# A masked-attention and rational-FFN kernel: a gate on weight loads, GpSimd planned as one queue, earlier norms, and a new table of order numbers

## The chip, the cores and the metric

The kernel runs on one core of a Trainium2 chip. Its time is the device time of one execution in microseconds, and the time of a version is the median of its runs. The core's engines run at the same time, each in the order of its own instruction list: TensorE (PE, with its weight loads PEld), VectorE (DVE), ScalarE (ACT), GpSimd (POOL), and SyncE (SP), which here only issues transfers. An instruction that must wait holds back all that stands behind it on its engine. Transfers are issued from the lists of SP, ACT and GpSimd, and the 16 DMA engines carry them out.

## The reference: what is computed

Eight batches with eight heads each, 576 positions and a head width of 64. In every row of scores only those within `tau` of the row's maximum take part in the softmax. The attention output, 4608 tokens by 512, goes through a two-layer network (512 to 2048 and back) whose nonlinearity is a rational function:

```python
scores = scale * np.matmul(q, k.transpose(0, 1, 3, 2))
thresh = np.max(scores, axis=-1, keepdims=True) - tau
scores = np.where(scores >= thresh, scores, -1000000000.0)
attn = np.exp(scores - np.max(scores, axis=-1, keepdims=True))
attn = attn / (np.sum(attn, axis=-1, keepdims=True) + 1e-09)
x = np.matmul(attn, v)          # then heads side by side: (4608, 512)
h = x @ w_in
P = a[0] + a[1] * h + a[2] * h * h + a[3] * h * h * h
Q = 1.0 + np.abs(b[0]) * np.abs(h) + np.abs(b[1]) * h * h
out = (P / (Q + 1e-06)) @ w_out
```

## The kernel before, in words

**The attention half.** Work goes in units: one pair of heads (32 pairs, four to a batch) and one tile of 128 query rows, or the last 64 rows of both heads. For each unit PE multiplies Q by K (L874 to L885), DVE takes the row maxima from PSUM (L891, L893), a small step on DVE or ACT makes the threshold (L900 or L898), ACT masks (L906) and exponentiates with a row sum (L910), DVE and ACT make the reciprocal (L915 or L917, then L921). Each probability row is then split into a high float16 half (`hi`, through the helper `times`, L341 on ACT or L343 on DVE) and a low one (L932, DVE). Both are transposed by DMA from SP (L942), and PE multiplies them with V (L1003). The first pairs go another way, with a float32 transpose on PE (L955, L960) and a copy out of PSUM (L333 or L335). The result, split into `x` high and `x` low (L1013 or L1015, L1019), is the input of the network.

**The network half.** It works on chunks of 256 tokens: two chunks to a batch, and one for the remainder rows of four batches. A chunk is done in steps of eight feature tiles (`moe_ops`). A step's first layer is L1248 on PE; ACT evacuates it (L1258); DVE and ACT evaluate the rational function (L1265 or L1267, L1273 to L1299); its value is scaled and split into a high half (L341 on ACT or L343 on DVE, with the scale `gsc`) and a low half (L1313, DVE); the second layer is L1322 on PE. The matmuls use float16 halves, three products for one.

**The norm chain.** Before the high and low halves of a chunk's first step can be made, the scale `gsc` of the chunk must be known, and it comes from a bound on the values. This is a chain over four engines, `norm_ops`, `bound`, `floor_ops`, `gain`: squares of `x` (L1107 on ACT or L1109 on DVE), a sum over them on PE (L1114), a maximum and a root on DVE (L1117, L452, L453), seven tiny instructions in a row on GpSimd (L1130 to L1136), two tiny ones on DVE (L1141, L1142), and two more on GpSimd (L1176 writes `gsc`, L1177; L1155 and L1156 for the first batch). Each has one value per partition. There are 18 such chunks, and 20 passes through the GpSimd part, since the chunks of the first batch are done for each half of the weights.

**GpSimd's list.** GpSimd does these tiny steps, clears some corners of the V tiles (L787), and issues the weight loads (L584, L634, 16 of them with 1 MB each) and, for the pairs from the ninth on, the loads of Q, K and V (L714 to L725, L758, L762), and most stores of the output (L1345, L1349). Its program order is one list.

**Who sets the order.** Nothing is ordered by hand. Every step is an `Op` with the engines that may do it, a cost on each, a key, and what it waits for; `Plan.order` lays all of them out on a model of the engines and so fixes, before anything runs, each engine's list and which engine does the flexible steps (`FLEX`, weighed by `START`, `EARLY` and `PRICE`). A key is the place of the unit or step plus a number from the table `K`. In the model before, GpSimd's arithmetic (`POOL`) and the transfers that it issues (`GD`) are two engines, though on the chip both stand in one list, and the two GpSimd parts of the norm chain cost 1.6 and 0.4. The norm chain of a chunk has the key of its first step less 0.1 (`norm_ops(ck, p - 0.1)`); a unit of the key is about one attention unit.

**The gate.** `decode_ops` holds back a weight load by an extra GpSimd instruction that reads the load `AHEAD` places earlier, if that one was issued less than `RECENT` before in the model; the condition is on L522. With `AHEAD = 3` and `RECENT = 9.0` it never applies, and no such instruction is in the program.

Of the kernel before, what the change touches and what calls it, by code (L numbers as in the profile page):

```python
# [30 lines left out]

LEAD, SPACE0, SPACING = 4.291, 6.563, 3.948
ENDK, ENDS = 2.754, 33.74

WHEN = [(-0.303, 2.09), (4.753, 1.193), (9.83, -0.311), (12.579, -0.299)]

V0, V1 = 2.109, -9.048

SINGLE = 18

# [3 lines left out]
LAST = (2, 0, 1)  # L44
SOON = 1

NB = 8
# [25 lines left out]

AHEAD_RANK = 3.973

AHEAD = 3

RECENT = 9.0

# [7 lines left out]

K = {"f1": 1.261, "f2": -0.32, "f4": -0.218, "f6": 0.826, "load": -1.146, "junk": 1.219, "sq": 0.474, "cn": -0.3, "cs": 0.443,
     "s1": 1.268, "s2": 0.713, "wh": 0.93, "wl": 0.588, "wc": -0.225, "vl": 0.197, "vc": 0.201, "vh": 0.137, "qk": 0.035,
     "max": -0.025, "thr": -0.477, "pre": -0.921, "sum": 1.315, "rec": -0.226, "rec2": 0.027, "diag": -1.496, "tr": 0.586,  # L90
# [4 lines left out]

SHIFT_STEPS, SHIFT_UNITS = {}, {}

START = {"ACT": 3.357, "DVE": 3.139}
START_END = 100.161
EARLY = {"ACT": 2.148, "DVE": 3.18}  # L100
EARLY_END = 1301.58
PRICE = {"ACT": 2.362, "DVE": 1.311}

TOL = {"PE": 0.11, "ACT": 0.025, "DVE": 0.0, "POOL": 0.1, "DMA": 0, "GD": 0}
WARM, WARM_END = 0.6, 400.0
# [29 lines left out]
class Plan:  # L135
# [21 lines left out]
    def op(self, eng, dur, key, fn, after=(), take=(), drop=()):  # L157
        engs = {eng: dur} if isinstance(eng, str) else eng
        o = Op(engs, key + self.shift, fn, [x for x in after if x is not None], list(take), list(drop))
        o.rank, o.tiling = self.rank, "ff"  # L160
        self.ops.append(o)
        return o
# [20 lines left out]
    def order(self):  # L183
# [21 lines left out]
        while left:  # L205
# [29 lines left out]
            t, o, e = best  # L235
# [13 lines left out]
            free[e] = end = t + o.dur  # L249
            busy[e] += o.dur  # L250
            if e == "PE":
                tiling = o.tiling[1]
# [39 lines left out]
def masked_attention_rational_ffn(  # L292
# [852 lines left out]
    def first_gain(ck, i, key):  # L1145
        j = index(ck)
        w = gt[:, j, :] if i == 0 else gt[:, NK + ck[2], :]

        def f():
            if i:  # L1150
                nc.gpsimd.tensor_scalar(w[:, 1:2], gt[:, j, 1:2], 1.0, 1.0, ALU.mult, ALU.mult)
            bound(w, isx[:, 0:1], sg[:, i:i + 1])

        def f_out():
            nc.gpsimd.tensor_scalar(gsc[:, j, i:i + 1], w[:, 5:6], 2.0 ** UPG, 1.0, ALU.mult, ALU.mult)  # L1155
            nc.gpsimd.tensor_scalar(osc_[:, j, i:i + 1], w[:, 4:5], su[:, 2 * NH + i:2 * NH + i + 1], 1.0, ALU.mult, ALU.mult)  # L1156
        plan.rank = key
        o = op("POOL", 1.6, key, f, [norm_done[ck], half_done[i]])
        return op("POOL", 0.4, key, f_out, [floor_ops(w, key, o)])

    def gain(ck, key):
# [16 lines left out]
        plan.rank = key  # L1178
        o = op("POOL", 1.6, key, f, [norm_done[ck], ready_all])
        return op("POOL", 0.4, key, f_out, [floor_ops(w, key, o)])  # L1180

# [24 lines left out]
    def moe_ops(ck, f0, nb, p, begins, ends, soon):  # L1206
# [11 lines left out]
        if ck not in norm_done:  # L1218
            norm_ops(ck, p - 0.1)
        if (ck, fh if first else 0) not in gsc_done:  # L1220
# [308 lines left out]
```

## Time and profile before

| | |
|---|---|
| median of 3 runs | 1341.53 us (1337.87 to 1342.36) |
| profiled execution | 1342.67 us |
| its span, first to last instruction | 1340.9 us |
| mean granted TensorE clock | 0.968 |
| HBM traffic | 63.25 MB read, 9.44 MB written |

The profiled execution lies 0.09% above the median, so sums made against it hold for the median as well; 1.8 us lie around its span. In the rows of the profile "busy" is time in which the engine works, and the waits are idle time put down to what ended it: "DVE gt L1141 <- POOL gt L1136: 35.0, 18, 3.7" says that DVE stood idle ahead of its instruction of line 1141 until the GpSimd instruction of line 1136 was done, 35.0 us in all, 18 times, at most 3.7 us. A timeline row gives start, duration, engine, line, and in brackets the idle time before it.

### The profile page before, as it was taken

The page shows a single profiled execution, that of the slowest core. Times are in us where ns is not written, and L with a number is a line of the kernel's source. Part 1 is how long each engine was busy: PE and PEld are TensorE (multiplying, and loading weights), DVE is VectorE, ACT ScalarE, POOL GpSimd, SP SyncE. Part 2 cuts the span into 40 slices and gives each one's busy share as a digit, 9 for nine tenths or more (in the row PEclk, how much of TensorE's full clock was granted, in tenths as well). Part 3 has the DMA queues.
Part 4 walks back from the last instruction along what each step waited for, and adds up shares of the span by engine and source line. Part 5 has one row for each costly group of instructions (what it writes and reads, how often), then busy time and mean ns, then how long its engine had stood idle before and what let it go on. Part 6 is the DMA issues. An engine that isn't in the chain of part 4 may idle for free.

```text
span 1340.9 us, 25552 instructions
## 1 busy us (share of the span) xinstructions
PE 1236.1 (92%) x9540; PEld 802.3 (60%) x9540; DVE 1220.4 (91%) x1789; ACT 1112.9 (83%) x2111; POOL 336.6 (25%) x663
## 2 busy tenths in 40 slices
PE   6689899999899989999999999989899999899996
PEld 5556656666566655565656565646565656566752
DVE  4699879999899899999999999989999999999875
ACT  3799778999899889888989798979889889896442
POOL 2010202013322331333224142142413441420110
PEclk8898989999999989999999999989899999999998
DMA  8253125568557865475545575566656875652000
GB/s 297 57 207 123 28 55 111 91 130 160 108 119 133 141 109 121 86 150 117 124 89 105 85 151 108 116 118 125 143 90 116 159 147 117 125 98 52 17 17 16
DMA packets 338987, 149.61 MB, mean 112 GB/s; under 512 B 314560, under 2 KB 320944, under 8 KB 338864
## 3 DMA queue, kind: packets, MB, share of 16 engines
q1 hardware_dynamic: 316240, 87.14, 37.1%
q0 software_dynamic: 22304, 60.25, 16.2%
q8 instruction: 75, 1.23, 0.4%
q10 hardware_dynamic: 320, 0.59, 0.2%
q14 instruction: 48, 0.39, 0.1%
HBM read 63.25 MB, written 9.44 MB: 54 GB/s over the span
## 4 chain that ended last, share of the span: by engine, by line
DVE 27%; PE 18%; ACT 7%; issue 6%; POOL 4%; DMA 3%; POOLq 0%; DVEq 0%; ACTq 0%
PE banks L1322 9%; DVE e L932 5%; PE banks L1248 5%; DVE st L891 4%; DVE t L1313 2%; DVE t L1299 2%; DVE t L1273 2%; DVE t L1291 2%; DMA pT<-e 2%; PE banks L1003 2%; DVE t L1287 2%; DVE t L1277 2%; PE banks L885 2%; DVE t L1295 1%; ACT e L906 1%
## 5 line engine op out<-in xcount | busy, mean ns | idle before, releaser
L1322 PE MATMUL banks<-wp,t 128*128 128x512 f16 x1728 | 408.8, 385 | 21.2 <-DVE t L1313 12.1
L1248 PEld LDWEIGHTS <-wi 128*128 128x128 f16 x3456 | 333.3, 98 | 116.6 <-issue 61.1
L1248 PE MATMUL banks<-x,wi 128*128 128x256 f16 x3072 | 366.3, 274 | 13.3 <-ACT t L1258 11.2
L1322 PEld LDWEIGHTS <-t 128*128 128x128 f16 x1728 | 163.5, 99 | 241.5 <-issue 45.9
L906 ACT ACTIVATE e<-banks,st 128x576 f32<-128x576 f32 x288 | 208.4, 734 | 24.0 <-DVE st L900 16.0
L910 ACT ACTIVATE e<-e,cf 128x576 f32<-128x576 f32 x288 | 221.4, 775 | 0.1
L932 DVE SCALAR_TENSOR_TENSOR e<-e,st,hi 128x576 f16<-128x576 f32 x252 | 204.6, 812 | 3.3 <-ACT hi L341 2.8
L891 DVE TENSOR_REDUCE st<-banks 128x2 f32<-128x1152 f32 x128 | 172.6, 1348 | 23.1 <-PE banks L885 22.9
L341 ACT ACTIVATE hi<-e,st 128x576 f16<-128x576 f32 x220 | 166.9, 766 | 23.7 <-DVE st L921 18.2
L885 PE MATMUL banks<-KK,QQ 64*128 64x512 f32 x512 | 150.3, 665 | 0.0
L1003 PE MATMUL banks<-pT,V 128*64 128x256 f16 (+1 forms) x2520 | 120.0, 249 | 7.4 <-DMA pT<-e 4.9
L1003 PEld LDWEIGHTS <-V 128*64 128x64 f16 x2520 | 104.9, 111 | 31.8 <-issue 26.4
L1258 ACT ACTIVATE t<-banks,hsc 128x512 f32<-128x512 f32 (+1 forms) x192 | 106.8, 574 | 15.5 <-PE banks L1248 9.7
L1280 ACT ACTIVATE t<-t,co 128x1024 f32<-128x1024 f32 (+2 forms) x69 | 81.4, 1180 | 23.9 <-DVE t L1287 23.4
L1291 DVE SCALAR_TENSOR_TENSOR t<-t,co,t 128x1024 f32<-128x1024 f32 (+2 forms) x69 | 91.3, 1324 | 8.2 <-ACT t L1283 8.2
L714 POOL DMA_DIRECT2D QQ<-in_qT_dram x47 | 26.0, 554 | 288.9 <-PE banks L885 155.3
L1313 DVE SCALAR_TENSOR_TENSOR t<-t,gsc,t 128x1024 f16<-128x1024 f32 (+2 forms) x69 | 91.4, 1325 | 5.5 <-ACT t L341 5.4
L1299 DVE SCALAR_TENSOR_TENSOR t<-t,co,t 128x1024 f32<-128x1024 f32 (+2 forms) x69 | 91.3, 1324 | 0.1
L1277 DVE SCALAR_TENSOR_TENSOR t<-t,co 128x1024 f32<-128x1024 f32 (+2 forms) x69 | 91.4, 1324 | 0.0
L1273 DVE SCALAR_TENSOR_TENSOR t<-t,co 128x1024 f32<-128x1024 f32 (+2 forms) x69 | 91.4, 1324 | 0.0
L1287 DVE SCALAR_TENSOR_TENSOR t<-t,co,t 128x1024 f32<-128x1024 f32 (+2 forms) x69 | 91.3, 1323 | 0.1
L341 ACT ACTIVATE t<-t,gsc 128x1024 f16<-128x1024 f32 (+2 forms) x45 | 53.6, 1192 | 45.2 <-POOL gsc L1176 25.5
(187 smaller groups left out, 1667.8 us busy)
## 6 DMA issues: line engine op xcount, KB each, us to landing
KK<-in_kT_dram POOLq DMA_DIRECT2D x94, 144.0 KB, 3.7
t<-in_w_in_dram POOLq DMA_DIRECT2D x8, 1024.0 KB, 8.6
t<-in_w_out_dram POOLq DMA_DIRECT2D x8, 1024.0 KB, 7.9
QQ<-in_qT_dram POOLq DMA_DIRECT2D x47, 144.0 KB, 3.3
V<-in_v_dram POOLq DMA_DIRECT2D x24, 256.0 KB, 4.6
out_dram<-u POOLq DMA_DIRECT2D x24, 256.0 KB, 3.4
QQ<-in_qT_dram POOLq DMA_DIRECT2D x47, 128.0 KB, 3.6
KK<-in_kT_dram SPq DMA_DIRECT2D x24, 144.0 KB, 3.0
```

Source lines behind the costliest of these rows:

```text
L341: nc.scalar.activation(dst, src, AF.Identity, scale=factor)
L885: nc.tensor.matmul(d, QQ[r, t * P:(t + 1) * P], KK[r, REM:S], **one)
L891: nc.vector.tensor_reduce(box["st"][:, 0:2], box["both"], AX.X, ALU.max, negate=True)
L906: nc.scalar.activation(ev(hh), box["s"][hh], AF.Prelu, scale=SCALE, bias=box["st"][:, 2 + hh:3 + hh], alpha=STEEP)
L910: nc.scalar.activation(e, e, AF.Exp, scale=passes, accum_out=box["st"][:, 4 + hh:5 + hh])
L932: nc.vector.scalar_tensor_tensor(box["lo"][:, c], ev(hh), box["st"][:, 6 + hh:7 + hh], box["hi"][:, c], ALU.mult, ALU.subtract)
L1003: nc.tensor.matmul(dst, V[:, c * P + head * D:c * P + (head + 1) * D], rhs, start=c == 0 and n == 0, stop=c == NT and n == 2)
L1248: nc.tensor.matmul(d, wi_tile(c, f0 + j, hl), x[:, c, :], start=c == 0 and n == 0, stop=c == NC - 1 and n == 2)
L1273: nc.vector.scalar_tensor_tensor(cols("r", x), h, a2, h, ALU.add, ALU.mult)
L1277: nc.vector.scalar_tensor_tensor(q, q, bc, q, ALU.add, ALU.mult)
L1313: nc.vector.scalar_tensor_tensor(gl, cols("r", x), gscale, gh, ALU.mult, ALU.subtract)
L1322: nc.tensor.matmul(acc[tt], g[x][:, o:o + P], wo_tile(f, y), start=begins and j == n == 0, stop=ends and j == nb - 1 and n == 2)
```

## The change

It has five parts, all of them in what the planner is told; no step computes anything else.

1. **Gate.** `AHEAD` goes from 3 to 2 and `RECENT` from 9 to 30, so that 12 gate instructions now stand in GpSimd's list: each holds back a weight load until the one two places ahead of it has landed.
2. **One queue.** In `Plan.order`, `POOL` and `GD` now share one time at which they are free.
3. **Costs.** The GpSimd parts of the norm chain are planned at 4.2 and 0.9 instead of 1.6 and 0.4.
4. **Norms earlier.** The chain's key is the step's less 1.797 instead of less 0.1.
5. **The table.** Nearly all planner numbers are new: `K`, the spacing of the steps, the weights for choosing an engine, and a small shift for every step and unit (`SHIFT_STEPS`, `SHIFT_UNITS`, empty before).

```diff
-AHEAD_RANK = 3.973
-AHEAD = 3
-RECENT = 9.0
+AHEAD_RANK = 2.613
+AHEAD = 2
+RECENT = 30.0
...
-     "o": 2.129, "st": 3.705}
-SHIFT_STEPS, SHIFT_UNITS = {}, {}
+     "o": 1.252, "st": 5.028}
+SHIFT_STEPS = {0: -0.034, 1: 0.283, 2: -0.3, 3: 0.255, 4: 0.121, 5: 0.344, 6: -0.243, 7: -0.637, 8: -0.352, 9: -0.422, 10: 0.497,
...
+EARLIER = 1.797
...
             free[e] = end = t + o.dur
             busy[e] += o.dur
+            if e in ("POOL", "GD"):
+                free["POOL"] = free["GD"] = end
...
-        o = op("POOL", 1.6, key, f, [norm_done[ck], half_done[i]])
-        return op("POOL", 0.4, key, f_out, [floor_ops(w, key, o)])
+        o = op("POOL", 4.2, key, f, [norm_done[ck], half_done[i]])
+        return op("POOL", 0.9, key, f_out, [floor_ops(w, key, o)])
...
         if ck not in norm_done:
-            norm_ops(ck, p - 0.1)
+            norm_ops(ck, p - EARLIER)
```

In the lists of the changed kernel most lines of the code stand 24 lines further down: its L1141 is the maximum of the norm chain (L1117 before), L476 and L477 are the root (L452, L453), L1165 and L1166 the two DVE steps behind GpSimd's part (L1141, L1142), L956 is L932, L1301 is L1277, L1323 is L1299, L1291 is L1267, L915 is L891, L359 is L335, L608 is L584, and L548 is the gate.

The first place is VectorE's list around the seventh pass through the chain, in the middle of the program. Before, `gt` is the tile of the norm chain, `e`, `hi` and `st` belong to attention units, and `t` to a step of the network:

```order
L932 SCALAR_TENSOR_TENSOR e_81<-e_81,st_89,hi_83 128x576
L1117 TENSOR_REDUCE gt<-banks 128x1
L452 TENSOR_SCALAR gt<-gt 128x1
L453 TENSOR_SCALAR gt<-gt 128x1
L932 SCALAR_TENSOR_TENSOR e_81<-e_81,st_89,hi_83 128x576
L891 TENSOR_REDUCE st_91<-banks 128x2
L1141 TENSOR_SCALAR gt<-gt 128x1
L1142 RECIPROCAL gt<-gt 128x1
```

In the changed kernel VectorE's list at the same pass reads:

```order
L1141 TENSOR_REDUCE gt<-banks 128x1
L476 TENSOR_SCALAR gt<-gt 128x1
L477 TENSOR_SCALAR gt<-gt 128x1
L956 SCALAR_TENSOR_TENSOR e_80<-e_80,st_89,hi_84 128x576
L956 SCALAR_TENSOR_TENSOR e_81<-e_81,st_90,hi_83 128x576
L359 COPY hi_83<-hi_83 128x64
L359 COPY e_81<-e_81 128x64
L1301 SCALAR_TENSOR_TENSOR t_72<-t_72,co 128x1024
L1291 TENSOR_SCALAR t_68<-t_71 128x1024
L915 TENSOR_REDUCE st_92<-banks 128x2
L1165 TENSOR_SCALAR gt<-gt 128x1
L1166 RECIPROCAL gt<-gt 128x1
```

Between the root and the step that needs GpSimd's seven instructions there stood two instructions, and now there are seven.

The second place is GpSimd's list at the start, the weight loads. Before, `t` are the tiles into which they go and `cf` is a scratch column:

```order
L520 TENSOR_SCALAR cf<-QQ_114 128x1
L584 DMA t_68<-in_w_in_dram 128x2x1024
L584 DMA t_69<-in_w_in_dram 128x2x1024
L584 DMA t_70<-in_w_in_dram 128x2x1024
L584 DMA t_71<-in_w_in_dram 128x2x1024
L634 DMA t_72<-in_w_out_dram 128x2x1024
```

GpSimd's list at the start of the changed kernel:

```order
L544 TENSOR_SCALAR cf<-QQ_114 128x1
L608 DMA t_68<-in_w_in_dram 128x2x1024
L608 DMA t_69<-in_w_in_dram 128x2x1024
L548 TENSOR_SCALAR cf<-t_68 1x1
L608 DMA t_70<-in_w_in_dram 128x2x1024
L548 TENSOR_SCALAR cf<-t_69 1x1
L608 DMA t_71<-in_w_in_dram 128x2x1024
L548 TENSOR_SCALAR cf<-t_70 1x1
L658 DMA t_72<-in_w_out_dram 128x2x1024
```

The first loads kept their order, and from the third on a gate stands ahead of each; of the 14 loads from the third on, 12 have one.

More of the change, by code (lines that the diff above doesn't have):

```diff
@@ L29 @@
 B2, B3, BA, B1, BH = [(0, 1, 2), (3, 4, 5)], [(0, 1, 2)], [(3,), (4,), (5,)], [(7,), (6,), (5,)], [(5,), (6,)]
[L32 to L39, printed above, removed]
+LEAD, SPACE0, SPACING = 4.211, 6.048, 3.976
+ENDK, ENDS = -0.095, 36.431
+WHEN = [(-0.353, 2.083), (4.745, 1.263), (9.569, -0.366), (12.731, -0.347)]
+V0, V1 = -1.222, -8.872
+SINGLE = 22
 VISITED = 8
@@ L86 @@
         "wh": {"ACT": 1.13, "DVE": 0.66}, "vc": {"ACT": 0.7, "DVE": 0.25}, "wc": {"ACT": 1.0, "DVE": 0.35}, "twice": {"ACT": 0.2, "DVE": 0.13}}
-K = {"f1": 1.261, "f2": -0.32, "f4": -0.218, "f6": 0.826, "load": -1.146, "junk": 1.219, "sq": 0.474, "cn": -0.3, "cs": 0.443,
-     "s1": 1.268, "s2": 0.713, "wh": 0.93, "wl": 0.588, "wc": -0.225, "vl": 0.197, "vc": 0.201, "vh": 0.137, "qk": 0.035,
-     "max": -0.025, "thr": -0.477, "pre": -0.921, "sum": 1.315, "rec": -0.226, "rec2": 0.027, "diag": -1.496, "tr": 0.586,
[4 rows of a table removed]
-SHIFT_STEPS, SHIFT_UNITS = {}, {}
[L98 to L104, printed above, removed]
+K = {"f1": 1.608, "f2": -0.599, "f4": -0.225, "f6": 0.208, "load": -2.04, "junk": 0.851, "sq": 3.176, "cn": -1.982, "cs": 0.511,
+     "s1": 0.805, "s2": -3.572, "wh": 1.301, "wl": 1.179, "wc": -1.565, "vl": 0.642, "vc": 0.731, "vh": 0.603, "qk": 0.278,
+     "max": -2.281, "thr": -0.0, "pre": -1.193, "sum": 2.158, "rec": 0.622, "rec2": -0.026, "diag": -1.94, "tr": -0.032,
[4 rows of a table added]
+SHIFT_STEPS = {0: -0.034, 1: 0.283, 2: -0.3, 3: 0.255, 4: 0.121, 5: 0.344, 6: -0.243, 7: -0.637, 8: -0.352, 9: -0.422, 10: 0.497,
[3 rows of a table added]
+SHIFT_UNITS = {0: -0.261, 1: -0.804, 2: 0.111, 3: -0.307, 4: -0.22, 5: 0.668, 6: 0.399, 7: -0.073, 8: -0.453, 9: 0.11,
[16 rows of a table added]
+START = {"ACT": 3.606, "DVE": 3.576}
+START_END = 116.646
+EARLY = {"ACT": 2.301, "DVE": 3.943}
+EARLY_END = 1205.603
+PRICE = {"ACT": 7.478, "DVE": 0.487}
+TOL = {"PE": 0.228, "ACT": 0.024, "DVE": 0.098, "POOL": 0.1, "DMA": 0, "GD": 0}
 WARM, WARM_END = 0.6, 400.0
@@ L1178, in gain @@
         plan.rank = key
-        o = op("POOL", 1.6, key, f, [norm_done[ck], ready_all])
-        return op("POOL", 0.4, key, f_out, [floor_ops(w, key, o)])
+        o = op("POOL", 4.2, key, f, [norm_done[ck], ready_all])
+        return op("POOL", 0.9, key, f_out, [floor_ops(w, key, o)])
     half_done = []
```

25 rows, old and new, of tables (K, SHIFT_STEPS, SHIFT_UNITS) are left out of this document.

## The prediction

> **What bounds the kernel now.** I read the engines' shares first, then the same by stage, then the waits of each stage, then the timeline of one wait. The first two:
>
> ```profile
> PE 1236.1 (92%) x9540; PEld 802.3 (60%) x9540; DVE 1220.4 (91%) x1789; ACT 1112.9 (83%) x2111; POOL 336.6 (25%) x663
> ```
>
> ```profile
> core 0: us, PE busy (x) PEld busy (x) DVE busy (x) ACT busy (x) POOL busy (x), PEclk, DMA share, GB/s
> 0.00:120.00 120.00, 91.73 (x548) 63.06 (x549) 87.34 (x195) 89.69 (x168) 14.73 (x38) 0.86 0.57 191
> 120.00:240.00 120.00, 110.36 (x854) 78.06 (x852) 104.39 (x193) 99.16 (x189) 19.20 (x45) 0.96 0.28 59
> 240.00:1200.00 960.00, 907.12 (x7312) 582.54 (x7309) 916.69 (x1313) 856.54 (x1674) 288.75 (x560) 0.98 0.63 120
> 1200.00:1341.00 141.00, 126.94 (x834) 78.62 (x832) 111.98 (x91) 67.52 (x84) 13.89 (x20) 0.98 0.13 28
> ```
>
> PE and DVE are both nearly full, and DVE's work alone is 1220 us. So the time is DVE's work plus its idle time, as long as PE can keep up. DVE's idle time by stage is stretch less busy: 32.7 us to 120 us, 15.6 to 240, 43.3 to 1200, 29.0 to the end. The waits say what it is made of, first in the long middle (240 to 1200 us), where ACT's row shows the next step of the same chain:
>
> ```profile
> DVE gt L1141 <- POOL gt L1136: 26.6, 14, 3.7
> DVE st L891 <- PE banks L885: 3.7, 7, 1.1
> ```
>
> ```profile
> ACT t L341 <- POOL gsc L1176: 17.7, 6, 5.2
> ```
>
> Of DVE's 43.3 us, 26.6 are one wait in the norm chain: GpSimd's seven tiny instructions. It comes 14 times, about 1.9 us each. The next cause has 3.7 us. ACT then waits another 17.7 us for the scale that the chain ends in. One of the 14 in the timeline, DVE's and GpSimd's rows:
>
> ```profile
> 670.40 0.15 DVE L453 TENSOR_SCALAR gt<-gt 128x1 int32<-128x1 int32 x1
> 670.47 0.81 DVE L932 SCALAR_TENSOR_TENSOR e<-e,st,hi 128x576 f16<-128x576 f32 x1
> 671.20 1.28 DVE L1273 SCALAR_TENSOR_TENSOR t<-t,co 128x1024 f32<-128x1024 f32 x1
> 672.41 1.27 DVE L1277 SCALAR_TENSOR_TENSOR t<-t,co 128x1024 f32<-128x1024 f32 x1
> ...
> 675.69 0.15 DVE L1141 TENSOR_SCALAR gt<-gt 128x1 int32<-128x1 int32 x1 [2.01 <-POOL gt L1136]
> ```
>
> ```profile
> 670.75 1.79 POOL L1130 TENSOR_SCALAR gt<-gt,isx,sg 128x1 f32<-128x1 f32 x1 [3.11 <-DVE gt L453]
> 672.64 1.29 POOL L1131 TENSOR_SCALAR gt<-gt,co 128x1 f32<-128x1 f32 x1
> 674.04 0.28 POOL L1132 TENSOR_SCALAR gt<-gt 128x1 f32<-128x1 f32 x1
> ...
> 675.44 0.22 POOL L1136 TENSOR_SCALAR gt<-gt 128x1 f32<-128x1 f32 x1
> ```
>
> GpSimd starts 0.2 us after the root, takes 4.9 us, and DVE has only three instructions to do meanwhile, to 673.68. That a stretch without this wait can be full shows here, where 240 to 280 us has no pass through the chain and 440 to 480 us has one of 3.7 us:
>
> ```profile
> 240.00:280.00 40.00, 40.00 (x292) 24.91 (x290) 39.97 (x52) 38.02 (x70) 2.07 (x3) 1.00 0.57 99
> 440.00:480.00 40.00, 35.34 (x260) 21.91 (x260) 35.74 (x61) 35.02 (x70) 14.84 (x33) 0.91 0.79 141
> ```
>
> With the stall, PE loses 4.7 us and DVE 4.2 us of the 40, and the granted clock falls to 0.91.
>
> **The change, term by term.** The sum is made against the profiled execution, 1342.67 us, 0.09% above the median of the runs.
>
> *The middle.* New order and costs put 4.5 to 6 us of DVE's work between root and L1141 in nearly every pass, where there were 1.5 to 3.5; at the place quoted from VectorE's list two instructions become seven. By the rows above and the two below the seven are 2 x 0.81 + 2 x 0.17 + 1.27 + 0.71 + 1.35 = 5.3 us.
>
> ```profile
> L891 DVE TENSOR_REDUCE st<-banks 128x2 f32<-128x1152 f32 x128 | 172.6, 1348 | 23.1 <-PE banks L885 22.9
> L1267 DVE TENSOR_SCALAR t<-t 128x1024 int32<-128x1024 int32 (+2 forms) x10 | 7.1, 711 | 2.8 <-ACT t L1258 2.8
> L335 DVE COPY e<-e 128x64 f16<-128x64 f16 x5 | 0.9, 172 | 0.0
> ```
>
> Against a chain of 4.9 us that would be no wait at all. But the chain is not of fixed length. In the timeline L1130 ends with DVE's L1273 (672.54 against 672.48) and L1131 soon after L1277, while the five that run with DVE idle take 0.2 to 0.35 us. Where DVE was idle throughout, the whole chain took 2.7 us:
>
> ```profile
> 1269.08 0.15 DVE L1141 TENSOR_SCALAR gt<-gt 128x1 int32<-128x1 int32 x1 [2.68 <-POOL gt L1136]
> ```
>
> So DVE's two-operand steps hold GpSimd up, and work put in between lengthens what it is to hide. The maximum over PSUM (L891) doesn't seem to: at the quoted place the chain has its 1.35 us for three of the seven, and one more may pass after each of three or four two-operand steps. I take six of seven done when the cover ends, and so 0.8 us of wait left (bounds 0 and 1.6) instead of 1.9: 14 x 1.1 = 15 us saved, bounds 4 and 26.6.
>
> The Trainium skill, SBUF — State Buffer, section "SBUF: two separate sides", calls the port pair that VectorE and GpSimd share an exclusive lock, held for a whole instruction, taken by a VectorE step with two SBUF inputs against a GpSimd step that reads SBUF. The rows of L1130 and L1131 agree with it, and it speaks against this change. Without any passing between two locked steps only PSUM-source work would be cover; that case is the first rival below.
>
> ACT's 17.7 us go too, since DVE's work from root to the first use of the scale grows by about 3 us; ACT is 89% busy there (856.54 of 960), so this is cover for DVE and PE and no term of its own.
>
> *120 to 240 us.* The first chunk's scale was late as well:
>
> ```profile
> DVE gt L1141 <- POOL gt L1136: 3.4, 2, 2.3
> DVE t L1313 <- ACT t L341: 3.3, 1, 3.3
> ```
>
> In the new list the first use stands some 19 us of DVE's work behind the root, not 6. Both waits go, 6.7 us; I take 6, bounds 2 and 9 (PE and ACT stood idle there too).
>
> *The end.* The waits for GpSimd after 1200 us:
>
> ```profile
> DVE gt L1141 <- POOL gt L1136: 5.0, 2, 2.7
> ```
>
> The two late passes get one more instruction of 2.3 us and one of 0.7 us as cover. PE's work sets the end there: I take 2.5, bounds 0 and 6.
>
> *Work that moves.* Steps that ACT or DVE may do change sides:
>
> ```profile
> L343 DVE TENSOR_SCALAR hi<-e,st 128x576 f16<-128x576 f32 x32 | 16.5, 515 | 0.1
> L343 DVE TENSOR_SCALAR t<-t,gsc 128x1024 f16<-128x1024 f32 (+2 forms) x24 | 18.3, 761 | 0.6 <-POOL gsc L1176 0.3
> L900 DVE TENSOR_SCALAR st<-st,cf 128x2 f32<-128x2 f32 (+1 forms) x43 | 9.5, 223 | 0.1
> L917 DVE TENSOR_SCALAR st<-st 128x2 f32<-128x2 f32 (+1 forms) x47 | 7.6, 162 | 6.2 <-ACT e L910 6.1
> ```
>
> By the lists DVE gets 29 `hi` halves (+14.9 us) and 39 thresholds (+8.7), and gives up 13 scalings (-9.9) and 34 reciprocals' first halves (-5.5): +8.2. Squares of norms, copies and splits of V and a few decode steps leave it, 0.2 to 1.3 us each, some 20 of them: -6. I take +2, bounds -4 and +6. The net shift on ACT is within 10 us, hidden by its 17% of idle time. PE's matmuls are the same but for some fillers.
>
> *The gate and the start.* DVE's waits up to 120 us, and what the DMA queues did from 8 to 33 us, when the first seven weight loads were under way:
>
> ```profile
> DVE st L891 <- PE banks L885: 18.1, 3, 8.0
> DVE u L771 <- DMA V<-in_v_dram: 5.8, 1, 5.8
> ```
>
> ```profile
> q0 software_dynamic: 1845, 7.16, 78.7%
> q1 hardware_dynamic: 2372, 1.33, 18.9%
> ...
> V<-in_v_dram SPq DMA_DIRECT2D x2, 256.0 KB, 14.1
> ```
>
> A V load took 14.1 us because its queue (q1) and the weights' (q0) moved packets nearly one for one, the weights' far larger. Two loads under way keep q0 nonempty if landing one takes no longer than streaming two: 7.16 MB in 25 us is 3.6 us for each of the 1.05 MB loads, and the quickest landing is
>
> ```profile
> DMA to landing us min/median/max: 5.4/8.6/16.0
> ```
>
> 5.4 us after issue, less than 7.2. So the gate hardly thins the weights, and V comes no sooner: 0, with bounds of 8 us gained (the stalls at 29 and 35 us shortened) and 6 lost (weights later). The Trainium skill, DMA: Bandwidth & Descriptors, section "Queues, rings and completion order", says an engine goes round its queues packet by packet; then depth doesn't matter as long as the queue isn't empty, which agrees with q0 and q1. Behind a gate on GpSimd's list stand only further weight loads, two clearings of V and the first bounds; decode steps on ACT and DVE wait for those loads.
>
> Sum: 1342.67 - 15 - 6 - 2.5 + 2 - 0 = 1321.2; I put it at **1321 us**, 1.6% below the profiled execution.
>
> **The rivals.**
>
> *GpSimd stays locked out.* Every two-operand step in the gap lengthens the chain by its own length, and only PSUM-source work is cover: 1.35 us in ten of the 14 passes, as before, so that the middle gains 4 us and the late chunks little. 1342.67 - 4 - 5 - 1 + 2 = 1335. For it: L1131 once took 2.55 us, over two such steps in a row. Against: more of DVE's steps in the gap means more ends at which GpSimd gets through. Chance 0.18.
>
> *All of it, and the clock.* Every wait of the chain goes, the start gains 8 us, and PE no longer drops to half clock behind the stalls, as it did here:
>
> ```profile
> 472.00:476.00 4.00, 4.00 (x10) 1.62 (x11) 4.00 (x6) 3.47 (x8) 1.03 (x2) 0.50 0.80 156
> ```
>
> 1342.67 - 26.6 - 8 - 6.7 - 5 + 2 = 1298, and I put the case at 1300. Against: the other 16.7 us of DVE's idle time in the middle have many causes that a new order can as well lengthen. Chance 0.12.
>
> *The stall moves.* The new list was laid out on a model; where its times are off, DVE waits as long at other places. 1341. Chance 0.08.
>
> *Slower: the gates hold up the decode.* GpSimd waits at 12 gates and each gated load lands later; ACT and DVE reach its decode step in order and stop, with attention behind it. If a gate costs g us of its load, the start grows by up to 12 g; beyond g = 1.9 this exceeds the 21.5 us gained. At 2.7 us a gate it is 32 us, 1353. For it: ACT's list now has the third load's decode ten places sooner. Against: after the seventh load the free tiles, not the queue, set the loads. Chance 0.10.
>
> **How the numbers follow.** My forecast has 0.52, its own range 1311 to 1330. A measurement of this kernel can tell about 0.3%, 4 us. Faster than 1337.5: the forecast, the second rival and nine tenths of the first, 0.80. The same: the moved stall and the rest of the first, 0.10. Slower: 0.10. The range 1302 to 1339 leaves out the slower rival and part of the second and third.
>
> **What would show it.** In the profile after: the wait of L1165 (L1141 before) for GpSimd 8 to 14 us in all instead of 35.0; GpSimd's instructions in the chain longer, ending with DVE's; DVE busy about 1222 us and its idle share down to 7%; the first V loads still landing after 12 us or more. A wait for GpSimd of 25 us or more shows the lock-out; an idle DVE of over 45 us before 120 us, behind decode steps, shows the gates. Wrong altogether would be a chain without wait and a time as before: then DVE did not bound the middle.

## The result and the profile after

| | before | after |
|---|---|---|
| median | 1341.15 us (1337.87 to 1342.36, 4 runs) | 1300.57 us (1295.55 to 1302.4, 4 runs) |
| ratio of the two | | 0.9695, 95% interval 0.9663 to 0.9727 |
| profiled execution, its span | 1342.67, 1340.9 us | 1295.55, 1293.3 us |
| mean granted clock | 0.968 | 0.987 |

The change gained 40.6 us, 3.0%. I had forecast 1321 us, a gain of 21.5 us, in a range of 1302 to 1339. The direction was right, the size half of what came, and the result lies just below the range.

The engines' shares in the profile after:

```profile
PE 1220.3 (94%) x9472; PEld 784.6 (61%) x9472; DVE 1221.3 (94%) x1796; ACT 1110.3 (86%) x2103; POOL 371.7 (29%) x675
```

DVE has the same work as before (1220.4 us); what went is its idle time. The profiled execution after is the fastest of its four and lies 5 us below their median, so the profiles differ by 7 us more than the medians. The stages after, in the columns stretch, length, then busy time of PE, PEld, DVE, ACT and POOL with instruction counts, granted clock, DMA share and GB/s:

```profile
0.00:120.00 120.00, 100.98 (x667) 71.31 (x668) 93.16 (x203) 98.72 (x186) 19.37 (x50) 0.91 0.60 191
120.00:240.00 120.00, 111.46 (x869) 75.63 (x868) 117.81 (x212) 110.18 (x218) 28.20 (x47) 1.00 0.39 81
240.00:1200.00 960.00, 924.22 (x7441) 588.55 (x7439) 939.14 (x1323) 865.81 (x1667) 309.14 (x560) 1.00 0.62 120
1200.00:1293.30 93.30, 83.66 (x502) 49.12 (x499) 71.22 (x61) 35.55 (x34) 14.96 (x18) 0.96 0.06 18
```

Length less DVE's busy time is its idle time, and with the busy time the differences add up by arithmetic to the change in the span, -47.6 us. The stages are cut by time, so the work in them isn't quite the same (DVE's 939 us in the middle against 917):

| stage | DVE idle before | after | change | forecast |
|---|---|---|---|---|
| 0 to 120 us | 32.7 | 26.8 | -5.9 | 0 |
| 120 to 240 | 15.6 | 2.2 | -13.4 | -6 |
| 240 to 1200 | 43.3 | 20.9 | -22.4 | -15 |
| 1200 to the end | 28.9 | 22.1 | -6.8 | -2.5 |
| DVE's busy time | | | +0.9 | +2 |

The same kernel profiled a second time (the run e14_after_again, a span of 1299.1 us) has 28.6, 3.3, 23.2 and 22.0 us of DVE's idle time in the four stages. So a stage is known to some 2 us only.

The waits of DVE in the middle stage, 240 to 1200 us, after:

```profile
DVE gt L1165 <- POOL gt L1160: 8.7, 10, 1.5
DVE st L915 <- PE banks L909: 3.2, 4, 2.0
```

The wait for the chain there was 26.6 us, and now is 8.7. From 120 to 240 us it was 3.4 us, with 3.3 behind the scale, and one row is left:

```profile
DVE gt L1165 <- POOL gt L1160: 1.0, 1, 1.0
```

After 1200 us it was 5.0. The first row below is the largest wait there now, three late steps that wait for ACT's exponential:

```profile
DVE t L1315 <- ACT t L1307: 7.5, 3, 4.1
...
DVE gt L1165 <- POOL gt L1160: 1.2, 2, 0.8
```

ACT's wait for the scale in the middle was 17.7 us, and the prediction had it go altogether. Now it is:

```profile
ACT t L365 <- POOL gsc L1200: 8.1, 6, 2.4
```

At the start, DVE's waits up to 120 us were 18.1 us for PE's scores and 5.8 for V. Now the wait for the scores is short and that for V longer:

```profile
DVE u L795 <- DMA V<-in_v_dram: 13.3, 3, 5.8
DVE st L915 <- PE banks L909: 4.7, 1, 4.7
```

The pass whose list the section on the change shows, in DVE's timeline after (start, duration, engine, line, operation; the idle time before it in brackets):

```profile
442.55 0.15 DVE L477 TENSOR_SCALAR gt<-gt 128x1 int32<-128x1 int32 x1
442.62 1.54 DVE L956 SCALAR_TENSOR_TENSOR e<-e,st,hi 128x576 f16<-128x576 f32 x2
444.09 0.17 DVE L359 COPY hi<-hi 128x64 f16<-128x64 f16 x1
444.20 0.18 DVE L359 COPY e<-e 128x64 f16<-128x64 f16 x1
444.29 1.28 DVE L1301 SCALAR_TENSOR_TENSOR t<-t,co 128x1024 f32<-128x1024 f32 x1
445.49 0.69 DVE L1291 TENSOR_SCALAR t<-t 128x1024 int32<-128x1024 int32 x1
446.09 1.35 DVE L915 TENSOR_REDUCE st<-banks 128x2 f32<-128x1152 f32 x1
448.02 0.15 DVE L1165 TENSOR_SCALAR gt<-gt 128x1 int32<-128x1 int32 x1 [0.58 <-POOL gt L1160]
```

GpSimd's timeline at the same pass:

```profile
442.89 1.32 POOL L1154 TENSOR_SCALAR gt<-gt,isx,sg 128x1 f32<-128x1 f32 x1 [3.20 <-DVE gt L477]
444.32 1.95 POOL L1155 TENSOR_SCALAR gt<-gt,co 128x1 f32<-128x1 f32 x1
446.37 0.28 POOL L1156 TENSOR_SCALAR gt<-gt 128x1 f32<-128x1 f32 x1
446.75 0.34 POOL L1157 TENSOR_SCALAR gt<-gt,co 128x1 f32<-128x1 f32 x1
447.06 0.34 POOL L1158 TENSOR_SCALAR gt<-gt,co 128x1 f32<-128x1 f32 x1
447.49 0.19 POOL L1159 TENSOR_TENSOR gt<-gt 128x1 f32<-128x1 f32 x1
447.77 0.22 POOL L1160 TENSOR_SCALAR gt<-gt 128x1 f32<-128x1 f32 x1
```

L1154 and L1155 take 1.32 and 1.95 us, and the latter ends at 446.27, just after DVE's run of SBUF steps (to 446.18). L1156 to L1158 go through under the maximum over PSUM (446.09 to 447.44); L1159 and L1160 come behind it, with DVE idle. The chain takes 5.1 us here, and DVE has something to do for all but 0.58 us of it, near the forecast (0.8). Over all 20 passes the seven steps took 2.5 to 4.9 us before, 3.8 on average, and 3.4 to 6.6 after, 5.2 on average: the pass that the prediction shows was the longest before.

The stretch that showed the cost of a stall before, 440 to 480 us, had DVE busy for 35.74 of 40 us at a granted clock of 0.91. It has a pass again:

```profile
440.00:480.00 40.00, 33.80 (x275) 21.62 (x272) 39.11 (x67) 37.35 (x70) 13.57 (x26) 1.00 0.61 127
```

PE is idle there for 6.2 us, longer than before (4.7 us), and yet is granted the full clock. So the 0.91 before doesn't follow from PE's idle time in the stretch alone.

What the queues did from 8 to 33 us, after:

```profile
q0 software_dynamic: 1500, 5.82, 68.4%
q1 hardware_dynamic: 3188, 2.07, 30.0%
...
V<-in_v_dram SPq DMA_DIRECT2D x4, 256.0 KB, 8.4
```

The weights' queue q0 moved 5.82 MB instead of 7.16, and V landed after 8.4 us instead of 14.1 (the loads of K after 7.4 instead of 11.0). Here the forecast had expected nothing.

### The profile page after: what moved, and what is told of

It is laid out like the page before. It is cut to its first block, busy times and chain, and to the rows that moved or that the text cites. A ratio compares the mean times of both kernels' runs of the same rounds, so it can differ in the third digit from the quotient of the medians.

```text
span 1293.3 us, 25473 instructions
## 1 busy us (share of the span) xinstructions
PE 1220.3 (94%) x9472; PEld 784.6 (61%) x9472; DVE 1221.3 (94%) x1796; ACT 1110.3 (86%) x2103; POOL 371.7 (29%) x675
## 4 chain that ended last, share of the span: by engine, by line
DVE 49%; PE 19%; issue 9%; ACT 9%; POOL 7%; DMA 7%; SPq 0%; POOLq 0%; DVEq 0%; ACTq 0%
PE banks L1346 9%; DVE e L956 9%; DVE st L915 8%; PE banks L1272 4%; DVE t L1337 4%; DMA pT<-e 4%; DVE t L1315 4%; DVE t L1319 3%; DVE t L1311 3%; DVE t L1323 3%; DVE t L1297 2%; DVE t L1301 2%; DMA V<-in_v_dram 2%; ACT e L930 2%; PE banks L909 2%
## 5 line engine op out<-in xcount | busy, mean ns | idle before, releaser
L1346 PE MATMUL banks<-wp,t 128*128 128x512 f16 x1728 | 401.7, 383 | 10.4 <-DVE t L1337 6.0
L1272 PE MATMUL banks<-x,wi 128*128 128x256 f16 x3072 | 360.0, 273 | 7.9 <-ACT t L1282 4.3
L956 DVE SCALAR_TENSOR_TENSOR e<-e,st,hi 128x576 f16<-128x576 f32 x252 | 203.7, 812 | 0.3 <-ACT hi L365 0.3
L915 DVE TENSOR_REDUCE st<-banks 128x2 f32<-128x1152 f32 x128 | 173.1, 1353 | 8.4 <-PE banks L909 7.9
L365 ACT ACTIVATE hi<-e,st 128x576 f16<-128x576 f32 x191 | 145.8, 768 | 23.6 <-DVE st L945 21.1
L909 PE MATMUL banks<-KK,QQ 64*128 64x512 f32 x512 | 147.3, 649 | 0.0
L1323 DVE SCALAR_TENSOR_TENSOR t<-t,co,t 128x1024 f32<-128x1024 f32 (+2 forms) x69 | 91.5, 1325 | 0.1
L1301 DVE SCALAR_TENSOR_TENSOR t<-t,co 128x1024 f32<-128x1024 f32 (+2 forms) x69 | 91.3, 1325 | 0.0
L1319 DVE SCALAR_TENSOR_TENSOR t<-t,t 128x1024 f32<-128x1024 f32 (+2 forms) x69 | 87.2, 1265 | 0.1
```

The lines of the kernel that those rows point to most:

```text
L365: nc.scalar.activation(dst, src, AF.Identity, scale=factor)
L909: nc.tensor.matmul(d, QQ[r, t * P:(t + 1) * P], KK[r, REM:S], **one)
L915: nc.vector.tensor_reduce(box["st"][:, 0:2], box["both"], AX.X, ALU.max, negate=True)
L956: nc.vector.scalar_tensor_tensor(box["lo"][:, c], ev(hh), box["st"][:, 6 + hh:7 + hh], box["hi"][:, c], ALU.mult, ALU.subtract)
L1272: nc.tensor.matmul(d, wi_tile(c, f0 + j, hl), x[:, c, :], start=c == 0 and n == 0, stop=c == NC - 1 and n == 2)
L1346: nc.tensor.matmul(acc[tt], g[x][:, o:o + P], wo_tile(f, y), start=begins and j == n == 0, stop=ends and j == nb - 1 and n == 2)
```

## The experiments

Each run is compared with the kernel before on the same chip, whose median was 1342.0 to 1343.4 us. The first expectations set theory G (the gate shortened the start) against O (the order did), and theory A (the waits for the chain cost more than their own length) against B (they cost their length or less, and the new table took away other idle time); later ones speak of theory C, formed after the third run: the whole path from the norm's root to the scale has a price, whoever waits on it. T, in one of them, says that the table's numbers carry the gain by themselves.

### The gate alone, and the gate alone left out

The kernel after without the gate, and the kernel before with it:

```diff
-AHEAD = 2
+AHEAD = 3
-RECENT = 30.0
+RECENT = 9.0
```

```diff
-AHEAD = 3
+AHEAD = 2
-RECENT = 9.0
+RECENT = 30.0
```

> The changed kernel without its 12 gate instructions on GpSimd; every list is otherwise the same. Theory G, the gate shortened the start (DVE's idle time to 120 us fell from 32.7 to 26.8 us): without it the weights crowd the first V and K loads again, DVE idles some 33 us to 120 us and the time rises by about 6 us, to 1306. Theory O, the order did it: the time stays within 3 us of 1300.6 and DVE's idle time to 120 us at about 27 us.

> The kernel before with the gate alone (AHEAD 2, RECENT 30), all other lists unchanged. Theory G: 1341 falls by about 6 us, to 1335, with the first V loads landing in under 10 us. Theory O: 1341 within 3 us, or slower by up to 6 us where a decode step now waits for its load.

Without the gate the kernel after took 1303.36 us (ratio to before 0.9707, 0.9687 to 0.9727), 2.8 us more than with it, which the intervals don't separate; measured again, the kernel with the gate took 1302.41 (0.9708). In the profile the start shows theory G all the same: without the gate V landed after 13.1 us, and DVE's idle time up to 120 us was 31.9 us, against 26.8 and 28.6 with it and 32.7 before the change. The gate alone on the kernel before took 1334.2 us (0.9935, 0.9912 to 0.9957): 8 us faster, with 24.1 us of idle time at the start. The queues from 8 to 33 us in that run:

```profile
q0 software_dynamic: 1455, 5.63, 67.2%
q1 hardware_dynamic: 2863, 1.91, 28.4%
...
V<-in_v_dram SPq DMA_DIRECT2D x4, 256.0 KB, 8.3
```

So two loads under way do thin the weights, in both orders alike. Why that is worth 8 us in the old order and at most a few in the new one wasn't tried; what waits for V and K at that moment may decide it.

### One load under way

```diff
-AHEAD = 2
+AHEAD = 1
```

> The kernel after with one weight load under way instead of two; the lists are the same but for gates on GpSimd. Theory G (a load under way lengthens the landing of V and K by its share of the queues): V lands after 6 to 7 us instead of 8.4, DVE's waits for V fall from 13.3 to 8 to 11, 2 to 5 us faster than the kernel after. Rival (the weights' stream then has gaps and the decode of weights waits): V as above, but DVE and ACT wait for weights, 3 to 15 us slower.

1314.02 us (0.9788, 0.9761 to 0.9815), 13 us above the kernel after. The same stretch of the queues:

```profile
q0 software_dynamic: 1002, 3.91, 47.8%
q1 hardware_dynamic: 4336, 2.51, 40.1%
...
V<-in_v_dram SPq DMA_DIRECT2D x4, 256.0 KB, 5.4
```

V lands after 5.4 us, and DVE's waits for V fall from 13.3 to 4.9 us, but now the decode waits for weights. ACT's largest wait up to 120 us:

```profile
ACT wp L565 <- DMA t<-in_w_out_dram: 12.9, 5, 4.1
```

The rival holds. The landing of V by weight loads under way, up to seven, two, one, is 14.1 (13.1 in the new order), 8.4 (8.3 in the old order) and 5.4 us. Two take less time than one in the new order and than up to seven in the old; in the new order two and up to seven aren't separated.

### The chain that DVE doesn't wait for, in the old order

The two DVE steps behind GpSimd's part read a constant, so that the bound is left out of the scales:

```diff
-            p, q = w[:, 4:5], w[:, 5:6]
...
-            nc.vector.reciprocal(q, p)
+            c = fl[:, fl_n[id(w)], :]
...
+            nc.vector.reciprocal(c[:, 2:3], c[:, 1:2])
```

> The kernel before in its own order, but the two VectorE steps behind GpSimd's part of the norm chain read a constant column, so that VectorE no longer waits for GpSimd; the bound is left out of the scales, GpSimd still does its steps in the same places. The direct waits are 35.0 us. Theory A, the waits cost more than their own length (PE falls to half clock behind them, queues drain): the time falls by 35 to 45 us, to 1296 to 1306. Theory B, the waits cost about their own length or less, and the new table took away other idle time by itself: the time falls by 18 to 28 us, to 1313 to 1323, and DVE's idle time in the middle outside the chain stays near 17 us.

1338.15 us (0.9964, 0.9951 to 0.9978), 4.8 us faster, though a wait of 35.0 us had been taken away. It had moved. DVE's largest waits in the middle of this run:

```profile
DVE t L1322 <- ACT t L341: 8.3, 4, 2.6
DVE t L343 <- POOL gsc L1185: 6.7, 5, 2.4
DVE st L917 <- ACT e L910: 6.3, 4, 5.3
```

And ACT's wait for the scale, 17.7 us before:

```profile
ACT t L341 <- POOL gsc L1185: 24.9, 8, 6.3
```

GpSimd's seven steps take longer than before, 5.0 us on average instead of 3.8, with DVE now at work beside them. The scale is made behind them, so the next user of the scale waits instead. Neither A nor B was right. This is where theory C comes from.

### The chain that nobody waits for, in both orders

In addition the steps that scale and the outputs read a constant, so that the chain's scales are left out of the result:

```diff
-        gscale = gsc[:, index(ck), fh:fh + 1]
+        gscale = gk[:, fh:fh + 1]
...
-        oscale = osc_[:, index(ck), fh if first else 0:][:, 0:1]
+        oscale = gk[:, 0:1]
```

> The kernel before in its own order, with nothing waiting for GpSimd's part of the norm chain: VectorE's two steps behind it read a constant, and the steps that scale (L341, L343, L1313) and the outputs (L1336, L1330) take a constant scale; the real scales are still worked out in the same places, but left out of the result. Theory C, the whole way from the root to the scale is what costs, not VectorE's own wait, and it explains the change: the time falls by 30 us or more, to 1311 or less. Theory B, the chain explains about half and the new table the rest: it falls by 12 to 22 us, to 1319 to 1329.

> The changed kernel, with nothing waiting for the chain, as in the run on the kernel before (constant scales, the real ones left out of the result). What is left of the chain's waits there is 10.9 us on DVE and some 12 us on ACT for the scale. Theory C: it falls by 8 to 15 us, to 1286 to 1293. Theory B: within 5 us of 1300.6.

In the old order 1293.62 us (0.9636, 0.9597 to 0.9675), 48.7 us faster; in the new one 1293.11 us (0.9641, 0.9595 to 0.9687), 7.5 us faster than the kernel after. The stages of the old order with the free chain:

```profile
0.00:120.00 120.00, 90.17 (x544) 61.34 (x545) 86.94 (x197) 89.22 (x166) 14.73 (x38) 0.86 0.58 191
120.00:240.00 120.00, 116.17 (x936) 83.10 (x934) 113.96 (x206) 108.72 (x206) 27.43 (x45) 1.00 0.32 66
240.00:1200.00 960.00, 930.73 (x7550) 600.98 (x7546) 945.01 (x1334) 874.48 (x1704) 336.96 (x562) 1.00 0.64 122
1200.00:1292.60 92.60, 85.32 (x519) 51.06 (x517) 71.60 (x58) 39.54 (x38) 23.23 (x18) 0.95 0.06 18
```

DVE's idle time falls from 32.7, 15.6, 43.3 and 28.9 to 33.1, 6.0, 15.0 and 21.0 us. The chain costs the old order 48.7 us and the new one 7.5, give or take some 7 by the intervals, at the edge of what theory C gave. What the pair shows is that without the chain both orders take the same time: the medians lie 0.5 us apart, with some 8 us either way. Within that, the whole gain of the change hangs on the chain. That 48.7 less 7.5, 41.2 us, is the gain (40.6) follows from this by arithmetic and is no second measurement. The constant scales also change the numbers that the second layer multiplies; whether that moves the clock (0.981 and 0.983 granted here, 0.968 and 0.987 in the kernels before and after) wasn't tried.

### A longer and a shorter chain

Six more clamps at the end of GpSimd's part, in the kernel after:

```diff
-        g.tensor_scalar(p, p, 2.0 ** -100, 2.0 ** 100, ALU.max, ALU.min)
+        for _ in range(7):
+            g.tensor_scalar(p, p, 2.0 ** -100, 2.0 ** 100, ALU.max, ALU.min)
```

> The changed kernel with six more GpSimd instructions in each pass of the norm chain (the last clamp repeated, same values), the lists otherwise the same: the chain is about 2 us longer and DVE's wait for it goes from 10.9 us to some 35 to 40 us. Theory A: the time rises by 35 us or more, to over 1335. Theory B: it rises by 18 to 28 us, to 1319 to 1329.

1336.43 us (0.9953, 0.9934 to 0.9973): 36 us of the gain are gone again, in the new order, as theory A had it. DVE's wait over the whole run, 10.9 us in the kernel after:

```profile
DVE gt L1166 <- POOL gt L1161: 39.0, 16, 4.1
```

The other way, 22 GpSimd steps fewer, in the kernel after and in the kernel before (the lower bound on the sum is left out):

```diff
-        g.tensor_tensor(p, p, q, ALU.add)
-        g.tensor_scalar(p, p, 2.0 ** -100, 2.0 ** 100, ALU.max, ALU.min)
+        g.tensor_scalar(p, p, q, 2.0 ** 100, ALU.add, ALU.min)
...
-            if i:
-                nc.gpsimd.tensor_scalar(w[:, 1:2], gt[:, j, 1:2], 1.0, 1.0, ALU.mult, ALU.mult)
-            bound(w, isx[:, 0:1], sg[:, i:i + 1])
+            bound(w, isx[:, 0:1], sg[:, i:i + 1], gt[:, j, 1:2])
```

> The kernel after with a shorter chain on GpSimd: the last addition and the bounds on its sum are one instruction (the sum's lower bound is left out), and the copy of the root for each further half of a first step is left out: 22 GpSimd instructions fewer, no other list changed. With six more per pass the time rose by 36 us, and with a chain that nobody waits for it fell by 7.5. Theory C: a part of the 7.5 goes, 2 to 5 us faster than the kernel after (1296 to 1299), DVE's wait for the bound 10.9 us before, 5 to 8 now. Rival (what is left of the wait is the ends of DVE's own two-operand steps, not GpSimd's count of steps): within 1.5 us of the kernel after, wait 9 to 12.

> The kernel after with the shorter chain once more. By theory C 2 to 5 us below the kernel after on the same chip (1296 to 1299); by the rival within 1.5 us of it.

> The kernel after, unchanged, for the comparison on one chip: 1297 to 1304.

> The kernel before with the shorter chain on GpSimd (20 times one instruction for the last addition and the upper bound on its sum, the lower bound left out, and two copies less); no other list changed. Theory C: in the old order every pass waits for the chain, so 20 passes save the 0.34 us of a step and what follows from it: 8 to 14 us faster than the kernel before, DVE's wait for the bound 35.0 us before, 25 to 30 now. Rival (the chain's length is that of DVE's two-operand steps that hold GpSimd up, not its count of steps): within 4 us, wait above 32.

In the new order 1296.19 us (0.9653, 0.963 to 0.9675), and measured again 1298.41 (0.9678, 0.9648 to 0.9708), beside the kernel after at 1300.57 and, on that same chip, 1302.41 (0.9708, 0.9679 to 0.9736). Both times that is 4 us less. Each pair of intervals overlaps; the two differences of the ratios, 0.42% and 0.30%, have a mean of 0.36% with some 0.28% either way. It is the fastest version measured that still scales by its chain. DVE's wait over the whole run:

```profile
DVE gt L1165 <- POOL gt L1159: 8.0, 13, 1.6
```

In the old order 1336.46 us (0.9959, 0.9941 to 0.9977), 5.5 us faster by the ratio, with this wait:

```profile
DVE gt L1141 <- POOL gt L1135: 33.1, 17, 4.6
```

That is less than theory C gave (8 to 14 us, a wait of 25 to 30) and, with 3 to 8 us by its interval, not clearly more than the rival (4). Per step the price is the same in all three, as far as their noise can tell: 36 us over some 120 steps added, 0.3; 4 us over 22 taken away, 0.2; 5.5 over 22, 0.25. A step that runs freely takes 0.2 to 0.35 us.

### The table without the rules, and the rules without the table

Four kernels each undo or do one part. The kernel after with late norms:

```diff
-EARLIER = 1.797
+EARLIER = 0.1
```

> The changed kernel with the norm chain's key back at 0.1 ahead of the step (EARLIER 0.1), all else new; the order is laid out again. Theory C: the cover between root and scale shrinks, DVE's and ACT's waits for GpSimd go back up, and the time rises by 20 to 35 us, to 1321 to 1336. Theory B: it rises by less than 10 us, since the shared queue, the costs and the table carry it.

The kernel before with one queue, the new costs and early norms, but the old table and no gate:

```diff
+            if e in ("POOL", "GD"):
+                free["POOL"] = free["GD"] = end
...
-        o = op("POOL", 1.6, key, f, [norm_done[ck], ready_all])
+        o = op("POOL", 4.2, key, f, [norm_done[ck], ready_all])
...
-            norm_ops(ck, p - 0.1)
+            norm_ops(ck, p - 1.797)
```

> The kernel before with its own table and no gate, but one GpSimd queue, the costs 4.2 and 0.9 and the norms 1.797 ahead; the order is laid out again. Theory C: DVE's wait for the chain falls under 15 us and the time by 15 to 30 us, to 1311 to 1326. Theory B: the model without a table made for it gains less than 10 us, as new waits appear.

The kernel after with two queues and the old costs, the first two edits of that diff the other way round:

> The kernel after with the planner's old model of GpSimd: arithmetic and transfers as two queues, the chain's costs back at 1.6 and 0.4; the table, the gate and the early norms stay. Theory C (the whole path from the norm's root to the scale is the price, and each rule only matters through the list that it gives): the table was made for the other model, so the list differs on every engine; the time goes back by half or more, 1320 to 1340. Theory T (the numbers of the table carry the gain by themselves, the model of GpSimd is an aid for finding them): within 6 us of the kernel after, 1295 to 1307. DVE's wait for GpSimd's bound: over 15 us in all by C, about 11 by T.

The kernel after with empty tables of shifts:

```diff
-SHIFT_STEPS = {0: -0.034, 1: 0.283, 2: -0.3, 3: 0.255, 4: 0.121, 5: 0.344, 6: -0.243, 7: -0.637, 8: -0.352, 9: -0.422, 10: 0.497,
...
+SHIFT_STEPS, SHIFT_UNITS = {}, {}
```

> The kernel after with its two tables of shifts emptied (38 steps and 160 units back at their computed places); its other numbers, the model, the gate and the early norms stay. If the gain is that of the early norms with a truthful model, the shifts are fine trimming: 1300 to 1312. If the gain depends on where each small step stands, as the two kernels that kept one half of the change suggest (1333 and 1342), the time is 1320 to 1345, and the chain's wait on DVE stays low (under 15 us) while waits of half a us to 3 us appear at many other places.

| | median | ratio, interval | DVE busy | DVE idle in all | DVE's wait for the chain, 240 to 1160 us |
|---|---|---|---|---|---|
| before | 1341.15 | | 1220.4 | 120.5 | 26.4 |
| after | 1300.57 | 0.9695 | 1221.3 | 72.0 | 8.7 |
| late norms | 1333.2 | 0.994, 0.9915 to 0.9965 | 1232.1 | 99.1 | 4.2 |
| old table, new model | 1342.05 | 1.0006, 0.9981 to 1.003 | 1225.9 | 113.0 | 9.7 |
| two queues, old costs | 1363.18 | 1.0155, 1.0129 to 1.0181 | 1239.8 | 119.6 | 22.2 |
| no shifts | 1352.62 | 1.0072, 1.0046 to 1.0099 | 1238.9 | 106.8 | 11.5 |

The idle time is the profiled span less DVE's busy time. The two queues with the old costs bring the wait back, as theory C says, but its range of time (1320 to 1340) was too low, and DVE also got 18.5 us more work. In the other three the wait at the chain is low and the time is lost elsewhere. Beside their expectations, the late norms came out at theory C's time but not by its mechanism, since the wait fell to 4.2 us; the old table with the new model came out as theory B said; and the empty tables of shifts took longer than either expectation (1345 at most). Where the time goes shows in the kernel with the old table and the new model. DVE's largest wait after 1200 us in that run, 7.1 us in the kernel before and 7.5 in the kernel after:

```profile
DVE t L1293 <- ACT t L1285: 16.2, 6, 4.1
```

Its stages from 240 us:

```profile
240.00:1200.00 960.00, 908.87 (x7328) 582.79 (x7327) 926.38 (x1333) 852.89 (x1664) 310.54 (x558) 0.98 0.62 121
1200.00:1338.90 138.90, 120.51 (x769) 74.01 (x767) 99.38 (x75) 59.42 (x60) 16.37 (x20) 0.93 0.06 18
```

It gains 9.7 us of DVE's idle time in the middle (43.3 to 33.6) and 6.8 from 120 to 240 us, and gives 10.6 back at the end (28.9 to 39.5) and 5.5 in work that moved to DVE. So the rules alone do take most of the wait away, and earn nothing. The table, with the gate, gains nothing that 8 us of noise would show where the chain is free. By these rows what it adds is that the early norms cost nothing elsewhere: DVE's work stays at 1221 us, and the end stays full. Which of its numbers do that isn't known.

## Why the prediction was right in direction and half in size

**What bounds the kernel: nothing speaks against it.** PE and DVE were named. DVE's work is the same, so the gain had to show as its idle time; that alone doesn't prove DVE the limit.

**The step that failed is the price of the chain.** The sum counted 15 + 6 + 2.5 = 23.5 us for it, and nothing for the start. In the profile DVE's idle time fell by 22.4, 13.4 and 6.8 us in these three stages, 42.6 together, and by 5.9 at the start; the runs with the free chain say that the whole 40.6 us hang on the chain, to within some 8. The prediction read the price from the rows that name the chain: "14 x 1.1 = 15 us saved". For those rows it was near: 26.6 to 8.7 is 17.9 us; 6.7 to 1.0 is 5.7 where it had 6; 5.0 to 1.2 is 3.8 where it had 2.5. What it left out is idle time that the profile puts down to other releasers. ACT's wait for the scale was called "cover for DVE and PE and no term of its own", and the other 16.7 us of DVE's idle time in the middle were taken as unaffected. ACT's wait didn't go but fell from 17.7 to 8.1 us. And that other idle time fell too: in the middle from 16.7 to 12.2 us, from 120 to 240 us from 8.9 to 1.2, at the end from 23.9 to 20.9, together 15.2 us of the 26 by which the profile beats the forecast (19 by the medians). The run in which DVE doesn't wait for the chain shows why such a row is no price: with the wait taken away the same time is waited elsewhere, until the last user of the chain is free. How much of the 15.2 us follows the chain itself and how much is better filling by the table isn't separated; in the old order, freeing the chain took 7.1 us off such rows (DVE's idle time fell by 45.4 us, of which 38.3 were the rows of the chain).

**What the chain's wait was made of: only in part as read.** The prediction took the pass at 670 us for all 14 of the middle: GpSimd starts 0.2 us after the root, and the wait is its seven steps. But in five of the 14 GpSimd came late, 1.2 to 3.1 us after the root, with a transfer just ahead in its list; that is up to 8 of the 26.6 us. The longest wait, 3.7 us in the stretch shown as the cost of a stall, is such a pass. The root ended at 463.08; GpSimd had been waiting for 3.39 us ahead of an output store, by the profile for a step of ACT, and the chain came behind it. Its seven steps then took 2.5 us:

```profile
464.65 0.57 POOL L1345 DMA_DIRECT2D out_dram<-u  x1 [3.39 <-ACT st L915]
...
466.19 0.33 POOL L1130 TENSOR_SCALAR gt<-gt,isx,sg 128x1 f32<-128x1 f32 x1
...
468.51 0.22 POOL L1136 TENSOR_SCALAR gt<-gt 128x1 f32<-128x1 f32 x1
```

After the change one pass of the middle is late behind a transfer, by 1.0 us. Planning GpSimd as one queue may be the reason, but the kernel with empty tables of shifts keeps that rule and has three such passes, of up to 3.2 us.

**The gate: wrong, and inside its bounds.** "So the gate hardly thins the weights, and V comes no sooner: 0, with bounds of 8 us gained". V landed 5.7 us sooner, and DVE's idle time up to 120 us fell by 5.9 us, nearly all of which is gone in the profile without the gate. In the old order the gate is worth the full 8 us, in the new one 1 to 3, which the runs can't tell from nothing. The failing link was that two loads keep the queue nonempty: the quickest landing, 5.4 us, was set against 7.2 us of streaming for two loads, but the four loads of `w_in` from 8 to 33 us took 9.0 us at the median, and q0 ran nearly dry between loads. From 25 to 27 us the queues moved, after and before:

```profile
q1 hardware_dynamic: 743, 0.54, 102.6%
q0 software_dynamic: 23, 0.07, 10.3%
```

```profile
q0 software_dynamic: 137, 0.52, 79.2%
q1 hardware_dynamic: 135, 0.15, 25.7%
```

The Trainium skill's rule on the packet-wise round (DMA: Bandwidth & Descriptors, "Queues, rings and completion order") isn't against this: an engine goes round the queues that it has work for. Before, both queues had work and moved packet for packet; after, q0 had next to none in these 2 us.

**Work that moves: right.** +0.9 us against +2. Three small slips elsewhere in the prediction change nothing: at 7.16 MB in 25 us a load of 1.05 MB takes 3.7 us, not 3.6; 21.5 us over 12 gates are 1.8 us a gate, not 1.9; and 40 less 35.74 is 4.3, not 4.2.

**The length of the chain: right.** It grew as DVE's work was put beside it (on average from 3.8 to 5.2 us), and 10.9 us of wait are left, inside the 8 to 14 named. At the quoted pass five of the seven steps were done when DVE's work ended, not six, three of them under the maximum over PSUM. The lock between VectorE and GpSimd, which the Trainium skill (SBUF — State Buffer, "SBUF: two separate sides") states and the prediction weighed against the change, shows in the rows of L1154 and L1155. Since DVE has work meanwhile, it leaves this order no more than those 10.9 us of wait.

**The rivals.** "All of it, and the clock" came nearest in time (1300) and had 0.12: the middle's clock did rise from 0.98 to 1.00 and the start gained 5.9 us, yet the chain's wait isn't all gone. Whether the clock adds anything of its own wasn't tried, and DVE's ledger can't tell: it closes by arithmetic, and a slower PE would stand in it as idle time of DVE. GpSimd locked out (25 us or more of wait) and the gates that hold up the decode didn't happen, but the latter does with one load under way: 13 us. The stall that moves is what the old table with the new rules does: 1342.05 us, where the rival had 1341.

Of the signs named ahead, the wait of L1165, GpSimd's longer chain and DVE's busy time came out; DVE's idle share fell to 5.6%, not 7%, and V landed after 8.4 us, not 12.

## What to carry to other kernels

A chain of tiny steps over several engines costs more than the waits that name it: free its last user in an experiment before pricing it, since taking away the first wait only hands it on (4.8 us of 48.7 here). A wait that names a chain can also be lateness: look at when its first step began and what stood ahead of it. An order that a planner lays out from tuned numbers can't be judged rule by rule: here the rules without the table, and the table without the early norms, the new model of GpSimd or its shifts, lost some 33 us or more of a gain of 41; only the gate could be left out at little cost. How many large loads to keep under way is a number to try: too few starve their reader (13 us here), and too many hold up the small transfers beside them (8 us in the old order).

## What the runs showed of the hardware

- Seven GpSimd steps on one value per partition took 2.5 us with DVE idle and 3.4 to 6.6 us in the kernel after, with DVE's SBUF steps beside them: at one pass L1154 and L1155 took 1.32 and 1.95 us there, and with DVE idle L1160 took 0.22 us. While DVE reduced from PSUM, L1156 to L1158 took 0.28 to 0.34 us, as with DVE idle.
- With up to seven weight loads of 1 MB under way on GpSimd's queue, a V load of 256 KB from SP's queue landed after 14.1 us, with two after 8.4, with one after 5.4; the weights' queue moved 7.16, 5.82 and 3.91 MB in the same 25 us.
- Two queues with work moved packets nearly one for one (137 and 135 in 2 us), though those of one were far larger (0.52 and 0.15 MB).
